# A small marker transfer and a wait for it ahead of eleven key loads of a decode attention kernel

## The chip, the cores and the metric

The kernel runs on one core of a Trainium2 chip. The metric is device time in microseconds, as the median of several runs. A profile is one execution of the program, recorded by the hardware profiler; its times count from the first instruction of the span.

## The reference

Two attention layers, A and B, take one new token for each of 4 batch entries, and their results are set side by side. Each has its own query weights `wq`, key and value caches and output weights `wo`. A reads its whole cache of 8192 positions, B only the last `W` = 2048.

```python
q = (x @ wq).reshape(B, Sq, Hq, Dh).transpose(0, 2, 1, 3)      # 32 heads of 128
k = jnp.repeat(k_cache, rep, axis=1)       # 8 key heads, rep = 4; B: k_cache[:, :, Sk - W:, :]
v = jnp.repeat(v_cache, rep, axis=1)
scores = jnp.einsum("bhqd,bhkd->bhqk", q, k) * (Dh ** -0.5)
p = softmax(scores, axis=-1)
o = jnp.einsum("bhqk,bhkd->bhqd", p, v)
return o.transpose(0, 2, 1, 3).reshape(B, Sq, Hq * Dh) @ wo
```

All tensors are bf16. The caches are large, and each of their elements is used for 4 query heads only.

## The kernel before

The work is cut into 20 units. Units 0 to 3 are B's, one per batch entry, with all 8 key heads. Units 4 to 19 are A's, each with two key heads of one batch entry. Every unit has 4 MB of keys and 4 MB of values. `K_sb` and `V_sb` have two slots each, and unit u uses slot u % 2.

For a unit, PE (TensorE) transposes the keys (L283, 16 groups of four), and DVE and ACT copy the transposed groups from PSUM (L299). PE forms the scores from them (L322), with scores of the first half in one of two banks SA and of the second half in SB. DVE takes maxima and differences, POOL the maximum over partitions (L441), ACT the exponentials (L469). PE then multiplies the values of the unit before with its probabilities (L338), and DVE divides by the sums (L491 for B, L504 for A); the semaphore of that step is called `otr`. Two units make a turn, and PE, ACT and DVE run the turns as a hardware loop. In each turn the output weights of one group of heads, 1 MB in `Wo_sb`, are multiplied in (L396), and DVE adds the product to `oacc` (L404, semaphore `ocp`).

All large loads are issued by SP (SyncE) at L566, in one queue, in the order that the loop from L753 writes down: for u = 1 to 20, the keys of unit u, then the values of unit u - 1, and, where u is even and at least 6, the 1 MB for `Wo_sb`. SP takes its list strictly in order (`emit`, L799), and a wait of one entry holds back all that follow. A key load of B comes in two halves, a value load of B in four quarters of 1 MB (L719 to L726). A's loads are whole, 4 MB each (L748), apart from the last unit's. What an entry waits for is that its slot is free:

```python
w = [("T", tjob_idx[(u - 2, 8 * q + 7)])] if u >= 2 else []                                  # keys of B, L721
w = [("otr", u - 2)] if kind == "V" else [("otr", u - 3)] if u >= 2 * T0P else [("T", tjob_idx[(u - 2, NJ - 1)])]   # A, L729
op("sp", dma(Wo_sb[:, :, :].rearrange("p r n -> p (r n)"), src), waits=[("ocp", tn - 1)], inc=("wo", tn))           # L761
```

`("T", ...)` is a transposition of the unit that used the slot before. The wait of one of A's loads stands at a semaphore increment just ahead of the load (L741). After the last value load SP issues eight pieces of `Wl_sb`, the last group of output weights, and at the end the outputs.

A transfer's semaphore counts 16, and `DMA_KEYS` (L162) names the keys that count so. `values` (L779) gives each key its count.

Of the kernel before, what the change touches and what calls it, by code (L numbers as in the profile page):

```python
# [6 lines left out]
BF16 = mybir.dt.bfloat16  # L7
# [7 lines left out]
def bass_concat_heads__gqa_block_cached__sliding_block_cached__decode_kernel(  # L15
# [23 lines left out]
    NSEG = 4  # L39
# [20 lines left out]
    WQ = [A_wq, B_wq]  # L60
    WO = [A_wo, B_wo]
# [11 lines left out]
    with ExitStack() as es:  # L73
        block = es.enter_context(nc.Block())

        def sb(name, shape, dt):
            return es.enter_context(nc.sbuf_tensor(name, shape, dt))

        def ps(name, n):
            return es.enter_context(nc.psum_tensor(name, [128, n], F32))  # L80

        def sm(name):
            return es.enter_context(nc.semaphore(name))
# [34 lines left out]
        OL = sb("OL", [128, C, Bn], BF16)  # L118
        oacc = sb("oacc", [Bn, D], F32)
        osb = sb("osb", [Bn, 2, D], BF16)  # L120
        dummy = sb("dummy_t", [128, 2], F32)
        SA = [ps("SA0", 512), ps("SA1", 512)]
        SB = ps("SB", 512)
# [2 lines left out]

        names = ["k0", "k1", "kh", "v0", "v1", "vl0", "vl1", "vl2", "wl0", "wl1", "wl2", "wl3", "wl4", "wl5", "wl6", "wl7", "x0", "x1", "w0", "w1", "wo",
                 "out0", "out1", "out2", "Tq", "Td", "Ta", "S", "PV", "Ed", "Ea", "Eq", "vs", "sub", "exp", "otr", "otp",
                 "ocp", "Ef", "fin0", "fin1", "ar1", "SM", "msk", "pset", "setup", "pm0", "pm1", "oc", "ocB", "mkb", "perm", "rq"]
        sems = {n: sm("s_" + n) for n in names}  # L130

        K_sbf = K_sb.bitcast(F32)
# [4 lines left out]
        tjob_idx, qp_idx, xt_idx, perm_idx, ot_idx, ol_idx, opj_idx = {}, {}, {}, {}, {}, {}, {}  # L137

        def sem_of(key):
            t = key[0]  # L140
            if t in ("K", "Kh"):
                return sems["k%d" % (key[1] % 2)]
            if t in ("V", "Vh"):
                return sems["v%d" % (key[1] % 2)]
            if t == "T":
                j = jobs[key[1]]
                return sems["Tq" if j["turn"] is None else "Td" if j["eng"] == "dve" else "Ta"]
            if t == "pm":
                return sems["pm%d" % key[2]]
            if t == "KH":  # L150
                return sems["kh"]
            if t in ("VL", "WL", "x", "out", "fin"):
                return sems["%s%d" % (t.lower(), key[1])]
            if t == "WQ":
                return sems["w%d" % key[1]]
            if t == "E":
                if jobs[key[1]]["turn"] is None:
                    return sems["Eq"]
                return sems["Ed"] if jobs[key[1]]["eng"] == "dve" else sems["Ea"]
            return sems["vs" if t in ("max", "maxc", "sum", "rcp", "os") else t]  # L160

        DMA_KEYS = ("K", "Kh", "KH", "V", "Vh", "VL", "WL", "x", "out", "WQ", "wo")  # L162

        plan = {e: [] for e in ("sp", "pe", "act", "dve", "pool")}
        turn = [None]
# [1 line left out]
        def op(eng, fn, waits=(), inc=None, bump=None):  # L167
            waits = list(waits)
            if not (eng == "pe" and turn[0] is not None):
                waits = [w for w in waits if w is not None]  # L170
            t = turn[0] if eng == "pe" or (eng in ("dve", "act") and turn[0] is not None and turn[0] >= T0P) else None
            plan[eng].append(dict(fn=fn, waits=waits, inc=inc, turn=t, bump=bump))
# [391 lines left out]
        def dma(dst, src):  # L564
            def fn(e):
                return e.dma_start(out=dst, in_=src)  # L566
            return fn
# [34 lines left out]
        for u in range(NU):  # L602
# [8 lines left out]
            for tok in TOK:  # L611
# [15 lines left out]
                if odd and tok in AFTER:  # L627
                    kind = AFTER[tok][0]
# [56 lines left out]
        for c in range(NC):  # L685
            w = [("VL", vch_of[c])]
# [18 lines left out]
        op("act", lambda act: act.activation(out=osb[:, 0, H2:D], in_=halves[1], func=ACTF.Copy), waits=[("fin", 1)], inc=("Ef",))  # L705
        op("act", dma(out[:, 0, H2:D], osb[:, 0, H2:D]), waits=[("Ef",)], inc=("out", 2))

        def kv_load(kind, u):
            un = units[u]
            cache = (KC if kind == "K" else VC)[un["P"]]  # L710
            buf = K_sb if kind == "K" else V_sb
            slot = u % 2
            if kind == "K" and slot == 1 and u < L:
                op("sp", lambda sp: sp.sem_inc(sems["kh"], 16), bump=(sems["kh"], 16, ("KH", u)))
            if un["P"] == 1:
                base = cache[un["b"], 0, SK - W:SK, :]
                hw = SK * DH
                n = NT // NPART[kind]
                for q in range(NPART[kind]):  # L719
                    if kind == "K":  # L720
                        w = [("T", tjob_idx[(u - 2, 8 * q + 7)])] if u >= 2 else []  # L721
                    else:
                        w = [("otr", u - 2)] if u >= 2 else [("T", tjob_idx[(1, 1)])] if u else [("T", qp_idx[(1, NQP - 1)])]
                    heads = HKV // NPART[kind]
                    src = bass.AP(tensor=base.tensor, offset=base.offset + q * heads * hw, ap=[[n * DH, W // n], [hw, heads], [1, n * DH]])
                    op("sp", dma(buf[:, slot, q * n:(q + 1) * n, :], src), waits=w, inc=(kind if q == NPART[kind] - 1 else kind + "h", u, q))  # L726
                return
            base = cache[un["b"], 2 * un["gp"], :, :]
            w = [("otr", u - 2)] if kind == "V" else [("otr", u - 3)] if u >= 2 * T0P else [("T", tjob_idx[(u - 2, NJ - 1)])]  # L729
            if kind == "V" and u == L:  # L730
                c0 = 0
                for i, n in enumerate(VCH):
                    t0, t1 = c0 * TC, (c0 + n) * TC
                    src = bass.AP(tensor=base.tensor, offset=base.offset + t0 * DH, ap=[[NT * DH, 32], [32 * NT * DH, 4], [1, (t1 - t0) * DH]])
                    op("sp", dma(buf[:, slot, t0:t1, :].rearrange("p t d -> p (t d)"), src), waits=w, inc=("VL", i))
                    c0 += n
                return
            src = bass.AP(tensor=base.tensor, offset=base.offset, ap=[[NT * DH, 32], [32 * NT * DH, 4], [1, NT * DH]])
            sem = sem_of((kind, u))
            bump = 16 * (NPART[kind] - 1)  # L740
            op("sp", lambda sp: sp.sem_inc(sem, bump), waits=w, bump=(sem, bump, None))  # L741
            if kind == "K" and u == L:
                for h in range(2):
                    t0 = h * NTH
                    src = bass.AP(tensor=base.tensor, offset=base.offset + t0 * DH, ap=[[NT * DH, 32], [32 * NT * DH, 4], [1, NTH * DH]])
                    op("sp", dma(buf[:, slot, t0:t0 + NTH, :].rearrange("p t d -> p (t d)"), src), inc=(kind, u, 0) if h == 0 else ("KH", u))
                return
            op("sp", dma(buf[:, slot, :, :].rearrange("p t d -> p (t d)"), src), inc=(kind, u, 0))  # L748

        for P in (1, 0):  # L750
            op("sp", dma(V_sb[:, 1 - P, :, :].rearrange("p t d -> p (t d)"), WQ[P].rearrange("(p c) n -> p (c n)", p=128)), inc=("WQ", P))
        kv_load("K", 0)
        for u in range(1, NU + 1):  # L753
            if u < NU:
                kv_load("K", u)
            kv_load("V", u - 1)
            tn = u // 2
            if u % 2 == 0 and tn in pieces:
                P, q = pieces[tn]
                src = WO[P][q * C * DH:(q + 1) * C * DH, :].rearrange("(p r) n -> p (r n)", p=128)  # L760
                op("sp", dma(Wo_sb[:, :, :].rearrange("p r n -> p (r n)"), src), waits=[("ocp", tn - 1)], inc=("wo", tn))  # L761
            if u == 16:
                op("sp", dma(out[:, 0, D:2 * D], osb[:, 1, :]), waits=[("ocB", 0)], inc=("out", 1))
# [17 lines left out]
        for eng in plan:  # L781
            for o in plan[eng]:
# [5 lines left out]
                if o["inc"] is not None:  # L788
                    key = o["inc"]
                    sem = sem_of(key)  # L790
                    amt = 16 if key[0] in DMA_KEYS else 1
                    counters[sem.name] = counters.get(sem.name, 0) + amt
# [143 lines left out]
```

## Time and profile before

| What | Value |
|---|---|
| Median of 3 runs | 439.15 us (438.97 to 439.83) |
| Profiled execution, its own time | 438.96 us |
| Its span | 437.0 us |
| PE busy | 365.0 us, 84% |
| DVE, ACT, POOL busy | 210.0, 195.0, 27.7 us |
| SP's DMA queue | 184.56 MB, 99.1% of 16 engines' span |
| HBM read | 184.56 MB |
| PE waiting for a key load (L283) | 34.4 us, 9 times |

Busy times are of one execution and add up over stages. The queue's share is the time that its packets took on the 16 DMA engines, against 16 times the span. The slices of the page cut the span into 40 equal parts; a digit is the busy share in tenths. In SP's order of time each row has the start, the duration of the issue on SP (not of the transfer), the line and the tile loaded; in the list of issues the last figure is the time from issue to landing. In a wait's row stand the engine and line that waited, what it waited for, the sum in us, how often, and the longest. In a row of a stretch stand its limits and length, the busy time of PE, PEld, DVE, ACT and POOL, the granted clock, the DMA share and the GB/s.

### The profile page before, as it was taken

How to read it: one execution, taken by the hardware profiler on the slowest of the kernel's cores; microseconds unless marked ns; L12 is line 12 of the kernel's file. 1: busy time of each engine (PE TensorE's matmuls, PEld its weight loads, DVE VectorE, ACT ScalarE, POOL GpSimd, SP SyncE). 2: the span in 40 equal slices, each digit the busy share in tenths (PEclk: the TensorE clock that was granted, in tenths of full speed). 3: DMA queues.
4: the chain of work that ended last, by engine and by line, in shares of the span. 5: the costliest groups of instructions: out<-in, count | busy, mean ns of one | idle time of the engine just before them, and what ended most of it. 6: DMA issues, size and time to landing. Idle time of an engine off the chain costs nothing.

```text
span 437.0 us, 15525 instructions
## 1 busy us (share of the span) xinstructions
PE 365.0 (84%) x7174; PEld 337.9 (77%) x7184; DVE 210.0 (48%) x406; ACT 195.0 (45%) x249; POOL 27.7 (6%) x88
## 2 busy tenths in 40 slices
PE   0168898998998959895989598969868996989996
PEld 0158897997997949795979588868868886979975
DVE  0004455664564634563456247525643563455651
ACT  1024473573653625371634254434534462536530
POOL 6100000000000000000000000000100000000000
PEclk9999999999999988999999899989996999799999
DMA  8999999999999999999999999999999999999996
GB/s 340 430 421 421 429 412 430 418 439 412 445 432 432 424 438 432 432 432 432 432 432 429 432 432 430 431 433 432 410 454 432 432 432 432 432 432 411 447 407 255
DMA packets 10996, 184.73 MB, mean 423 GB/s; under 512 B 1236, under 2 KB 2280, under 8 KB 2408
## 3 DMA queue, kind: packets, MB, share of 16 engines
q1 hardware_dynamic: 10960, 184.56, 99.1%
q8 instruction: 8, 0.13, 0.1%
q14 instruction: 4, 0.03, 0.0%
q10 hardware_dynamic: 24, 0.01, 0.0%
HBM read 184.56 MB, written 0.01 MB: 422 GB/s over the span
## 4 chain that ended last, share of the span: by engine, by line
PE 54%; DMA 40%; issue 2%; DVE 1%; SPq 1%; ACT 1%
DMA K_sb<-in_A_k_cache_dram 29%; PE KT L283 27%; PE OT L338 11%; DMA K_sb<-in_B_k_cache_dram 7%; PE SB L322 5%; PE SA L322 4%; DMA V_sb<-in_A_v_cache_dram 4%; PE KT L396 4%; PE SA L350 1%; PE KT L338 1%; SPq L566 1%; DVE oacc L404 1%; PE KT L263 1%; ACT KT_sb L299 1%; DVE OS L501 0%
## 5 line engine op out<-in xcount | busy, mean ns | idle before, releaser
L283 PE MATMUL KT<-identf,K_sb 128*128 128x128 f32 x1280 | 207.6, 296 | 44.1 <-DMA K_sb<-in_A_k_cache_dram 30.7
L299 ACT ACTIVATE KT_sb<-KT 128x1024 bf16<-128x1024 bf16 (+1 forms) x192 | 165.1, 881 | 120.6 <-PE KT L283 120.6
L283 PEld LDWEIGHTS KT<-identf,K_sb 128*128 128x128 f32 x1280 | 147.6, 150 | 49.3 <-DMA K_sb<-in_A_k_cache_dram 31.7
L299 DVE COPY KT_sb<-KT 128x512 int32<-128x512 int32 x160 | 110.5, 691 | 132.1 <-PE KT L283 130.7
L338 PE MATMUL OT<-PT,V_sb 128*128 128x64 bf16 x2560 | 78.1, 193 | 1.6 <-issue 1.1
L338 PEld LDWEIGHTS OT<-PT,V_sb 128*128 128x128 bf16 x2560 | 75.9, 98 | 1.8 <-issue 1.2
L469 ACT ACTIVATE PT<-Dt 128x512 bf16<-128x512 f32 x40 | 24.6, 630 | 84.0 <-DVE Dt L458 84.0
L322 PEld LDWEIGHTS SA<-RQc,KT_sb 128*128 128x128 bf16 x1280 | 56.9, 98 | 2.3
L322 PEld LDWEIGHTS SB<-RQc,KT_sb 128*128 128x128 bf16 x1280 | 51.1, 97 | 7.9 <-issue 4.4
L322 PE MATMUL SA<-RQc,KT_sb 128*128 128x16 bf16 x1280 | 56.4, 170 | 0.0
L322 PE MATMUL SB<-RQc,KT_sb 128*128 128x16 bf16 x1280 | 52.9, 170 | 0.0
L420 DVE TENSOR_REDUCE M<-SB 128x8 f32<-128x512 f32 (+1 forms) x20 | 13.8, 692 | 50.0 <-PE SB L322 50.0
L441 POOL PARTITION_ALL_REDUCE MB<-M1m x20 | 7.7, 387 | 334.3 <-DVE M1m L434 334.3
L396 PE MATMUL KT<-Wo_sb,OL 128*4 128x512 bf16 x80 | 18.9, 379 | 0.0
L201 PE MATMUL KT<-ident,x_sb 4*128 4x4 bf16 x8 | 0.6, 170 | 19.9 <-POOL identf L537 19.9
L201 PEld LDWEIGHTS KT<-ident,x_sb 4*128 4x128 bf16 x8 | 0.4, 112 | 20.1 <-issue 20.1
L476 DVE TENSOR_REDUCE LB<-SA 128x8 f32<-128x512 f32 (+1 forms) x20 | 13.7, 684 | 2.8 <-PE SA L350 2.8
L458 DVE TENSOR_TENSOR Dt<-SA,MBm 128x512 f32<-128x512 f32 x20 | 13.8, 692 | 0.7
L367 DVE TENSOR_TENSOR ORx<-KT,MSK 32x1024 bf16<-32x1024 bf16 x10 | 12.1, 1211 | 3.3 <-PE KT L362 3.3
L458 DVE TENSOR_TENSOR Dt<-SB,MBm 128x512 f32<-128x512 f32 x20 | 13.6, 681 | 0.0
L420 DVE TENSOR_REDUCE M<-SA 128x8 f32<-128x512 f32 (+1 forms) x20 | 13.6, 681 | 0.0
L350 PE MATMUL SA<-PT,onesb 128*128 128x128 bf16 x168 | 12.7, 218 | 0.0
(69 smaller groups left out, 118.0 us busy)
## 6 DMA issues: line engine op xcount, KB each, us to landing
K_sb<-in_A_k_cache_dram SPq DMA_DIRECT2D x15, 4096.0 KB, 22.5
V_sb<-in_A_v_cache_dram SPq DMA_DIRECT2D x15, 4096.0 KB, 30.3
K_sb<-in_B_k_cache_dram SPq DMA_DIRECT2D x8, 2048.0 KB, 23.6
V_sb<-in_B_v_cache_dram SPq DMA_DIRECT2D x16, 1024.0 KB, 18.4
V_sb<-in_B_wq_dram SPq DMA_DIRECT2D x1, 4096.0 KB, 12.5
V_sb<-in_A_wq_dram SPq DMA_DIRECT2D x1, 4096.0 KB, 21.8
Wo_sb<-in_B_wo_dram SPq DMA_DIRECT2D x4, 1024.0 KB, 11.9
K_sb<-in_A_k_cache_dram SPq DMA_DIRECT2D x2, 2048.0 KB, 17.5
```

What stands on the lines that cost most here:

```text
L283: ins = pe.transpose(out=bkf[:, pi * 128:(pi + 1) * 128], in_=K_sbf[:, slot, t0:t0 + 2, :].rearrange("p t d -> p (t d)"), identity=identf[ ...
L299: ins = e.tensor_copy(out=d, in_=r) if eng == "dve" else e.activation(out=d, in_=r, func=ACTF.Copy)
L322: ins = pe.matmul(out=stb[:, t % NTH * C:(t % NTH + 2) * C], lhsT=ktv[:, pi, :, e], rhs=RQc[:, u % 2, t // TS, e, :], start=(e == 0), stop ...
L338: ins = pe.matmul(out=otb[:, s * NW:s * NW + w], lhsT=V_sb[:, slot, t, :], rhs=PT[:, slot, t * C:t * C + w], start=(j == 0), stop=(j == n ...
L350: ins = pe.matmul(out=SA[u % 2][:, s * NM:(s + 1) * NM], lhsT=onesb[:, :], rhs=PT[:, u % 2, c0:c0 + NM], start=(i == 0), stop=(i == n - 1))
L367: return dve.tensor_tensor(out=ORx[:, :, :, :], in0=bk[0:NR, 0:128].rearrange("p (i o r) -> p r o i", o=1, r=C).broadcast_to([NR, C, C, 12 ...
L396: ins = pe.matmul(out=bk[0:Bn, 0:D], lhsT=OL[:, i, :], rhs=Wo_sb[:, i, :], start=(i == 0), stop=(i == C - 1))
L420: return dve.tensor_reduce(out=M1[:, h * n:(h + 1) * n].rearrange("p (s h) -> p s h", h=C), in_=bank[:, :].rearrange("p (s j h) -> p s h j ...
L441: return pool.partition_all_reduce(MB[:, 0:n], M1m[:, 0:n], channels=128, reduce_op=ReduceOp.max)
L458: return dve.tensor_tensor(out=Dt[:, h * NTH * C:(h + 1) * NTH * C].rearrange("p (s j h) -> p s j h", s=Sh, h=C), in0=bank[:, :].rearrange ...
L469: return act.activation(out=PT[:, u % 2, a:b], in_=Dt[:, a:b], func=ACTF.Exp, scale=scale)
L476: return dve.tensor_reduce(out=LB[:, 0:n].rearrange("p (s h) -> p s h", h=C), in_=SA[u % 2][:, 0:NSEG * NM].rearrange("p (s j h) -> p s h ...
```

## The change

A new tile `rs_sb` of 16 rows of 32 elements (64 bytes a row, 1 KB) takes a small transfer from A's `wo`, which nothing reads. Its key is `rs`, on one semaphore. `mark(u)` puts it in SP's list for the units in `MARKS`; `passed()` gives the next key load a wait for it.

- Units 0 to 3: the marker goes ahead of the last quarter of the unit's values, and the next key load (of units 2 to 5) waits for it. For units 2 and 3 it is the first half of the keys that waits.
- Units 5, 7, 9, 11, 13, 15 and 17: the marker goes ahead of the entry for `Wo_sb`, its wait for `ocp` included, and the key load of the unit two later (7, 9, 11 to 19) waits for it. The load waits for the marker beside its old wait.

Key loads of units 6, 8, 10 to 18 have no marker. The order of all other transfers, and every other engine's list, is as before. The lines of the new kernel lie one further from the new tile on, and 17 further after `kv_load` and the loop.

```diff
+        rs_sb = sb("rs_sb", [16, 32], BF16)
...
-        DMA_KEYS = ("K", "Kh", "KH", "V", "Vh", "VL", "WL", "x", "out", "WQ", "wo")
+        DMA_KEYS = ("K", "Kh", "KH", "V", "Vh", "VL", "WL", "x", "out", "WQ", "wo", "rs")
...
+        MARKS = (0, 1, 2, 3, 5, 7, 9, 11, 13, 15, 17)
+        marked = []
+
+        def mark(u):
+            if u in MARKS:
+                op("sp", dma(rs_sb[:, :], WO[0][0:16, 0:32]), inc=("rs", u))
+                marked.append(u)
+
+        def passed():
+            return [("rs", marked.pop())] if marked else []
+
         def kv_load(kind, u):
...
                     if kind == "K":
-                        w = [("T", tjob_idx[(u - 2, 8 * q + 7)])] if u >= 2 else []
+                        w = ([("T", tjob_idx[(u - 2, 8 * q + 7)])] if u >= 2 else []) + passed()
                     else:
                         w = [("otr", u - 2)] if u >= 2 else [("T", tjob_idx[(1, 1)])] if u else [("T", qp_idx[(1, NQP - 1)])]
+                        if q == NSEG - 1:
+                            mark(u)
...
             w = [("otr", u - 2)] if kind == "V" else [("otr", u - 3)] if u >= 2 * T0P else [("T", tjob_idx[(u - 2, NJ - 1)])]
+            if kind == "K":
+                w = w + passed()
...
             if u % 2 == 0 and tn in pieces:
                 P, q = pieces[tn]
+                mark(u - 1)
                 src = WO[P][q * C * DH:(q + 1) * C * DH, :].rearrange("(p r) n -> p (r n)", p=128)
                 op("sp", dma(Wo_sb[:, :, :].rearrange("p r n -> p (r n)"), src), waits=[("ocp", tn - 1)], inc=("wo", tn))
```

More of the change, by code (lines that the diff above doesn't have):

```diff
@@ L128, in bass_concat_heads__gqa_block_cached__sliding_block_cached__decode_kernel @@
                  "out0", "out1", "out2", "Tq", "Td", "Ta", "S", "PV", "Ed", "Ea", "Eq", "vs", "sub", "exp", "otr", "otp",
-                 "ocp", "Ef", "fin0", "fin1", "ar1", "SM", "msk", "pset", "setup", "pm0", "pm1", "oc", "ocB", "mkb", "perm", "rq"]
+                 "ocp", "Ef", "fin0", "fin1", "ar1", "SM", "msk", "pset", "setup", "pm0", "pm1", "oc", "ocB", "mkb", "perm", "rq", "rs"]
         sems = {n: sm("s_" + n) for n in names}
```

## The prediction

> **What bounds the kernel now.** I read the page first, its slices and its DMA queues:
>
> ```profile
> span 437.0 us, 15525 instructions
> ...
> DMA  8999999999999999999999999999999999999996
> GB/s 340 430 421 421 429 412 430 418 439 412 445 432 432 424 438 432 432 432 432 432 432 429 432 432 430 431 433 432 410 454 432 432 432 432 432 432 411 447 407 255
> ...
> q1 hardware_dynamic: 10960, 184.56, 99.1%
> ```
>
> The DMA row is at 9 from the second slice to the last but one, and one queue, SP's, carries all of it. PE is busy for 84%. A queue that is never empty sets the end; every microsecond in which it runs dry is lost.
>
> The chain of waits puts 54% on PE, and its pieces are PE work without a break from 33.88 to 140 us. That is no contradiction: the chain follows a key load back to its issue, and the issue to PE, though the load then stood in the queue. So I looked at the order of time on SP, for one turn, and at SP's own waits:
>
> ```profile
> 159.25 0.54 SPq L566 DMA_DIRECT2D K_sb<-in_A_k_cache_dram  x1
> 159.89 0.55 SPq L566 DMA_DIRECT2D V_sb<-in_A_v_cache_dram  x1
> 183.97 0.33 SPq L566 DMA_DIRECT2D Wo_sb<-in_B_wo_dram  x1
> 184.48 0.54 SPq L566 DMA_DIRECT2D K_sb<-in_A_k_cache_dram  x1
> 185.12 0.55 SPq L566 DMA_DIRECT2D V_sb<-in_A_v_cache_dram  x1
> 201.46 0.54 SPq L566 DMA_DIRECT2D K_sb<-in_A_k_cache_dram  x1
> ```
>
> ```profile
> SPq L566 <- DVE oacc L404: 137.0, 6, 23.8
> SPq L741 <- DVE ON L504: 94.6, 6, 16.5
> ```
>
> K of unit 9, issued at 184.48, is needed at once but lands at 205.3, 20.8 us later. Its own 4.19 MB and the 1.05 MB of Wo before it take 9.74 + 2.5 us, so V of unit 7 had 8.5 us to go at the issue. That is the depth of the queue at its shallowest in a turn, and what the change spends. The rates come from two views, the stretch of the first loads and the issues:
>
> ```profile
> 13.30:23.00 9.70, 2.69 (x96) 2.67 (x97) 0.65 (x4) 0.78 (x4) 1.74 (x8) 1.00 1.00 429
> ```
>
> ```profile
> V_sb<-in_B_wq_dram SPq DMA_DIRECT2D x1, 4096.0 KB, 12.5
> V_sb<-in_A_wq_dram SPq DMA_DIRECT2D x1, 4096.0 KB, 21.8
> Wo_sb<-in_B_wo_dram SPq DMA_DIRECT2D x4, 1024.0 KB, 11.9
> ```
>
> Two 4 MB loads issued 0.44 us apart land 9.74 us apart (0.80 + 12.5 and 1.24 + 21.8): that is the price of 4.19 MB in a full queue. The first, into an empty queue, took 12.5, so start and completion together cost 2.76.
>
> The trace's records of single packets add the rest. A 32 KB packet takes 1.218 us, a 16 KB one 0.612, an 8 KB one 0.312, a 512 B one 0.026, a completion 0.009. The 16 engines do not run level: V of unit 7 ends between 190.46 and 192.65, a lag of 2.19 us which builds up over the first 58 us and then stands still.
>
> **What the Trainium skill says.** "DMA: Bandwidth & Descriptors", section "Queues, rings and completion order": on each engine a queue's descriptors are consumed in ring order, and the completion increment lands only after that engine's earlier writes. The trace agrees as far as it goes: loads land in the order of issue. The section "Why a DMA increments its semaphore by 16 and not by 1": the full count needs every engine that the transfer uses, and 16 rows use all 16. So the marker lands when the last engine has passed it. "Anatomy of one DMA": a semaphore is waited for on the issuing sequencer, not by the DMA engines, and a transfer has about 2 us fixed, mostly completion (a fit for another issue path). Here completion is shorter: 0.37 us from the last completion packet to the semaphore, at the first load and at the output alike.
>
> **The change, part by part.** *Removed:* nothing. *Added:* 11 transfers of 16 rows of 64 bytes, and 11 waits on SP. On each engine a marker is one small packet and a completion, 0.035 us by the 512 B row; I take 0.04, so 11 x 0.04 = 0.4 us, all on the stream that sets the end. Their issues (0.29 to 0.37 us on SP, as for the outputs) fall while SP has 9 us and more to spare: four just before a last V quarter, seven before a wait for L404.
>
> *Moved:* the key load, from the end of SP's other waits to the landing of the marker. In the turn shown that is from 184.48 to about 193.2. Behind it on SP stand V of unit 8 (then issued at about 193.9, with 12 us of K before it) and K of unit 10, which waits until 201.46 anyway. So nothing else is late, and the cost is what happens between marker and key load. From the passing of the last engine, at 192.69:
>
> - landing 0.37; SP's waking 0.02 to 0.13 (Wo goes out 0.02 after DVE's end; PE starts on K 0.13 after its semaphore), I take 0.08; one semaphore increment 0.10 (the gap between the issues at 184.48 and 185.12, less 0.54)
> - from the issue to the first packets 1.05 to 1.60 on fifteen engines at the first load (issued at 0.80, packets from 1.84 to 2.40)
> - sum: packets can start 1.6 to 2.15 us after the marker.
>
> On the last engine the short transfer (Wo, or a V quarter: both 8 packets of 8 KB) covers 8 x 0.312 = 2.50 us. So on the engine that sets the end the load comes 0.35 to 0.9 us before it is empty. The engines that are ahead by up to 2.19 us run dry, but that only uses up their lead.
>
> What no row shows is whether a load that comes so late joins without a gap. Into an empty queue, the first packets took 1.3 to 2.23 us in place of 1.218: 0.1 to 1.0 us of filling. Were all of that paid, full rate would begin 2.15 to 3.0 us after the marker, and since a load lands with its slowest engine, the stream would lose 3.0 - 2.5 = 0.5 us per marker. If filling hides behind the short transfer, it loses 0. Below nothing I see no way. I take 0.2, nearer to 0, since the requests are out while 8 KB packets still move. Then 11 x (0.2 + 0.04) = 2.6 us: the span goes from 437.0 to 439.6, and with 1.96 us around it (438.96 - 437.0) to 441.6 against the profiled execution. The median of the runs is 0.19 above that execution, so 441.8.
>
> The four markers of units 0 to 3 are no cheaper. PE runs behind the key loads there (no wait for K in the chain from 33.88 on), with K of unit 2 landed some 13 us before its turn, but their gaps stay in the stream and arrive at K of unit 7.
>
> **Rivals.** A difference under 0.2% (0.9 us) can't be told from none; 0.08 us per marker is the border.
>
> *Hidden*: the key load joins in time, only the packets cost: 439.15 + 0.4 = 439.6. For it speaks the 0.35 to 0.9 us in hand; against it the fill of up to 1.0. A marker that passed V out of turn would end here too, as the wait would never be the last.
>
> *Late*: the marker's completion takes the skill's 2 us in a loaded queue, not 0.37. Packets then start 3.25 to 3.8 after it, 0.75 to 1.3 past the cover; with 0.3 of filling I take 1.3 per marker: 11 x 1.34 = 14.7, so 453.9. Against it: 0.37 us for a load with the queue full behind it.
>
> *Faster*: bringing the engines level lets the B part move at the later rate. From 54 to 106 us the stretches moved 418, 422 and 428 GB/s, later ones about 431. B's 33.6 MB of K and V would take 77.8 us instead of 79.3 at 423, 1.5 us less, hence 438.1 with the packets. It decides from 428 GB/s on. Against it: the 8 KB packet costs 0.312 us where a quarter of a 32 KB one is 0.305, and the change leaves packets as they are. Nothing else could be faster: the stream has no gap to close.
>
> **How the numbers follow.** The restart cost at 0.08 to 0.5 per marker: 0.58, its own range 440.4 to 445.1. Hidden 0.29, late 0.08, faster 0.05. The range holds the first two and a little past the upper bound, 438.8 to 446.5, which leaves out faster and late, 0.13, and some of the uncertainty of the bounds. Slower 0.58 + 0.08 = 0.66, same 0.29, faster 0.05.
>
> **What would show it.** SP's waits have a row of some 11 waits for the marker's DMA, about 8 to 9 us each, and L404 stays beside it. The marked key loads land about 12 us after issue, not 21 to 23; the unmarked ones stay above 20. Wo goes out at about the old times plus the gaps so far. The queue's share falls from 99.1% to 97 or 98%, as leading engines stand still. The lag at the end of a load, 2.2 us now, falls below 1.5. The landings of K of units 7, 9, 11 and 13 are now 41.3 us apart (164.0, 205.3, 246.7, 288.0); I expect 41.4 to 41.8, hidden shows no more than 41.4, late 42.6. PE's idle time before K grows by what the stream loses. I am wrong if the gap on the last engine is not what I bound: the fill under load is the unmeasured term.

## The result

The changed kernel takes 461.21 us (median of 6 runs, 454.9 to 465.29), the kernel before 439.19 (438.97 to 439.83). The ratio is 1.043, with a 95% interval from 1.035 to 1.050; it leaves out the two longest runs of the changed kernel, one of which is the profiled one. The forecast was 441.8, in a range up to 446.5. So the direction was right and the size was not: 22 us by the medians and 19 by the ratio, in place of 2.6, and single runs that lie 10 us apart, where those of before lie within 1.

The page of the kernel after, with the lines that answer to those shown of before (span, share of the DMA engines and GB/s in 40 slices, SP's queue):

```profile
span 460.5 us, 15538 instructions
...
DMA  9999999999999999989998999899999979997995
GB/s 365 403 424 418 379 417 367 418 372 402 403 430 433 387 433 424 441 356 436 430 436 362 445 421 409 339 436 436 382 407 416 450 291 444 416 450 306 431 425 211
...
q1 hardware_dynamic: 11312, 184.57, 95.3%
```

Before, nearly all slices from the fourteenth on were at some 430 GB/s; now one in each turn falls to between 291 and 387. The same bytes flow at about the same rate between these dips. SP's waits of the kernel after:

```profile
SPq L567 <- DVE oacc L405: 146.1, 6, 25.0
SPq L757 <- DMA rs_sb<-in_A_wo_dram: 94.8, 9, 16.7
...
SPq L823 <- DMA rs_sb<-in_A_wo_dram: 36.8, 2, 22.3
```

The markers are waited for 11 times, as expected, and the row for Wo's wait for DVE is still there. SP's order of time in the turn of unit 11, and the issues with their time to landing, after and before:

```profile
234.59 0.35 SPq L567 DMA_DIRECT2D Wo_sb<-in_B_wo_dram  x1
244.16 0.54 SPq L567 DMA_DIRECT2D K_sb<-in_A_k_cache_dram  x1
244.84 0.54 SPq L567 DMA_DIRECT2D V_sb<-in_A_v_cache_dram  x1
252.11 0.54 SPq L567 DMA_DIRECT2D K_sb<-in_A_k_cache_dram  x1
```

```profile
K_sb<-in_A_k_cache_dram SPq DMA_DIRECT2D x15, 4096.0 KB, 15.0
V_sb<-in_A_v_cache_dram SPq DMA_DIRECT2D x15, 4096.0 KB, 24.0
```

```profile
K_sb<-in_A_k_cache_dram SPq DMA_DIRECT2D x15, 4096.0 KB, 22.5
V_sb<-in_A_v_cache_dram SPq DMA_DIRECT2D x15, 4096.0 KB, 30.3
```

The key load goes out 9.6 us after Wo here (8.8 to 9.7 over the seven turns), where the prediction has about 9.2. But it then takes longer to land: the row's 15.0 is the median of marked and unmarked loads together, and the marked ones of units 7 to 17 take 13.2 to 15.0 us, where about 12 was forecast. Where the missing time is, the trace's records of landings say. In a full queue 4 MB of keys land 9.72 us after the load ahead of them, and the half load of unit 19 4.9. Behind Wo, in the seven marked turns of A, they land later by 2.05, 1.2, 2.95, 2.15, 3.05, 2.8 and 2.5 us, 16.7 in all; behind a last quarter of B's values by 1.65, 2.75, 0.55 and 1.55, 6.5 in all. Together 23.2 us, and the span has grown by 23.5. All other loads land at the old distance. The loss is at the eleven places of the change and nowhere else, but it is 2.1 us at each, not 0.2, and it varies.

### The profile page after: what moved, and what is told of

It reads as the page before. It is cut to its first block, busy times and chain, and to the rows that moved or that the text cites. A ratio compares the mean times of both kernels' runs of the same rounds, so it can differ in the third digit from the quotient of the medians.

```text
span 460.5 us, 15538 instructions
## 1 busy us (share of the span) xinstructions
PE 368.0 (80%) x7174; PEld 340.3 (74%) x7184; DVE 209.9 (46%) x406; ACT 195.0 (42%) x249; POOL 27.6 (6%) x88
## 3 DMA queue, kind: packets, MB, share of 16 engines
q1 hardware_dynamic: 11312, 184.57, 95.3%
## 4 chain that ended last, share of the span: by engine, by line
DMA 54%; PE 24%; PEld 15%; issue 4%; SPq 2%; PEldq 1%; DVE 0%; ACT 0%
DMA rs_sb<-in_A_wo_dram 30%; DMA K_sb<-in_A_k_cache_dram 12%; PE KT L284 11%; DMA K_sb<-in_B_k_cache_dram 7%; PEld KT L284 7%; PE OT L339 5%; DMA V_sb<-in_A_v_cache_dram 5%; PEld OT L339 3%; PEld SA L323 2%; SPq L567 2%; PEld SB L323 2%; PE SB L323 2%; PE SA L323 2%; PE KT L339 1%; PEldq L905 1%
## 5 line engine op out<-in xcount | busy, mean ns | idle before, releaser
L284 PE MATMUL KT<-identf,K_sb 128*128 128x128 f32 x1280 | 209.9, 298 | 62.7 <-DMA K_sb<-in_A_k_cache_dram 49.0
L284 PEld LDWEIGHTS KT<-identf,K_sb 128*128 128x128 f32 x1280 | 149.5, 151 | 68.2 <-DMA K_sb<-in_A_k_cache_dram 50.1
```

Of the source, the lines that this page charges most:

```text
L284: ins = pe.transpose(out=bkf[:, pi * 128:(pi + 1) * 128], in_=K_sbf[:, slot, t0:t0 + 2, :].rearrange("p t d -> p (t d)"), identity=identf[ ...
```

## The experiments

Three words are used from here on. The *cover* is the work that stands in the queue behind the marker, in us of transfer: what the engines still have to do once the marker has passed. The *restart* is the time from the marker's passing of the last engine until the key load runs at full rate. *Late* is how much later than in a full queue the key load lands, counted from Wo's landing.

Theory 1 is the one of the prediction: a wait spends the depth of the queue, and what is lost is the restart less the cover that the short transfer gives. Its rivals: the small transfers disturb the stream; a wait for all 16 engines has a price of its own, whatever the cover.

**Markers without waits.** The markers stay, each in its own columns of a larger tile; no load waits for one.

```diff
-            return [("rs", marked.pop())] if marked else []
+            return []
```

> All eleven markers go out where the change puts them (each into its own columns of the tile), but no key load waits for one. Theory 1 (the wait spends the queue's depth; what is lost is the time from the marker's passing to the key load at full rate, less the cover of the short transfer): no wait, no loss, only 11 x 0.04 us of packets, 439.2 to 440.0. Rival, the small transfers themselves disturb the stream (2 us each): the time of the changed kernel, 455 to 465.

Measured: 439.36 us, ratio 1.0003 (0.9995 to 1.0012). The markers themselves cost nothing that can be measured, not even the 0.4 us that I gave them.

**Only A's seven markers.**

```diff
-        MARKS = (0, 1, 2, 3, 5, 7, 9, 11, 13, 15, 17)
+        MARKS = (5, 7, 9, 11, 13, 15, 17)
```

> Only the seven markers of layer A (units 5 to 17), with their waits; the four of layer B and their waits are gone. In the profile of the changed kernel the seven landings of a key load behind Wo come 1.2 to 3.1 us late, 16.7 in all, the four of B 0.5 to 2.8, 6.4 in all. Theory 1: the losses add up, so 439.2 + 16.7 = 456, within 452 to 459. Rival, B's markers bring the engines out of step once and A only inherits it: below 446.

Measured: 454.26 us (450.81 to 456.76), ratio 1.032 (1.026 to 1.039). The losses add up. The rest of the study works with these seven, since they all stand in the same place.

**Twice the cover.** The value load ahead of Wo is issued in two parts, with the marker between.

```diff
+            if kind == "V" and u in MARKS:
+                for i, (t0, t1) in enumerate(((0, 3 * NT // 4), (3 * NT // 4, NT))):
...
+                    if i == 0:
+                        mark(u)
```

> A's seven markers as in the run with these alone, but the value load ahead is cut in 3/4 and 1/4, and the marker stands between the parts: behind it come 1 MB of values and 1 MB of Wo, 4.9 us of cover in place of 2.5. Theory 1 with a slowest engine that is back at full rate 2.5 + 2.4 = 4.9 us after the marker: 0 to 0.4 us per marker, 439.2 to 442. Rival, a wait for all 16 engines costs its 2.4 us however deep the queue is: 454 to 459.

Measured: 440.03 us, ratio 1.0024 (1.0015 to 1.0033). SP still waits seven times for a marker:

```profile
SPq L757 <- DMA rs_sb<-in_A_wo_dram: 47.5, 7, 8.1
```

Yet the six whole key loads land 9.71 to 9.73 us after Wo, and the half load 4.90, as in the kernel before. So the wait as such costs nothing; the depth behind it decides.

**No cover.** The marker moves behind Wo.

```diff
-                mark(u - 1)
                 src = WO[P][q * C * DH:(q + 1) * C * DH, :].rearrange("(p r) n -> p (r n)", p=128)
                 op("sp", dma(Wo_sb[:, :, :].rearrange("p r n -> p (r n)"), src), waits=[("ocp", tn - 1)], inc=("wo", tn))
+                mark(u - 1)
```

> A's seven markers behind Wo instead of ahead of it: nothing in the queue covers the key load. Theory 1: each loses 2.5 us more, 7 x (2.4 + 2.5) = 34 us, 473 (465 to 478). Rival, a price per wait whatever the cover: 454 to 459. If only one late engine makes the loss at 2.5 us of cover, and all restart alike from an empty queue, about 7 x 3.2 = 22 us, 462.

Measured: 462.01 us (461.88 to 463.03), ratio 1.053. That is 3.3 us per marker, and the key loads land 2.8 to 3.6 us late, 3.1 in the mean. Theory 1 in its plain form wanted 473. Four stretches of one microsecond in this run, around one marker, and SP's issue there:

```profile
242.00:243.00 1.00, 1.00 (x24) 0.98 (x22) 0.33 (x2) 0.73 (x1) 0.00 (x0) 1.00 0.42 165
243.00:244.00 1.00, 1.00 (x24) 0.99 (x21) 0.65 (x1) 0.66 (x2) 0.00 (x0) 1.00 0.00 0
244.00:245.00 1.00, 1.00 (x19) 0.64 (x17) 0.00 (x0) 0.66 (x1) 0.00 (x0) 1.00 0.73 197
245.00:246.00 1.00, 1.00 (x40) 1.00 (x39) 0.48 (x1) 0.00 (x0) 0.00 (x0) 1.00 0.79 328
```

```profile
243.43 0.54 SPq L567 DMA_DIRECT2D K_sb<-in_A_k_cache_dram  x1
```

For a whole microsecond nothing moves. This measures the restart by itself: from the passing of the last engine to the marker's landing 0.62 us; SP 0.07; from the issue to the first packets 1.3 us on the first engines and 1.5 to 2.3 on the others, often in two groups of eight; and the early packets take 1.7 to 2.2 us instead of 1.21. The engines end the load within 0.25 to 1.0 us of each other.

The sum, 3.1, leaves 0.6 with 2.5 us of cover. But there 2.2 was lost. The packet records of the run with 2.5 us of cover show why. From the second marker on mostly one engine is late: 15 engines end the key load close together, and the last one 1.2 to 2.5 us after them. In the turn of unit 11 the last Wo packet ends at 240.88, fifteen first key packets begin from 240.33 to 240.94, and the sixteenth begins at 242.46 and takes 2.35 us. The records do not name the engine of a packet, but the turn of unit 13 in the changed kernel leaves one only: fifteen first key packets begin from 289.98 to 290.21, while the sixteenth engine is still at its last Wo packet, which ends at 290.51, and its own first key packet begins at 291.78 and takes 2.13. So the late engine is the one that was last with Wo. In the turns of these two kernels in which it is over a microsecond behind, its first key packet begins 0.8 to 2.4 us after its last Wo packet. From this comes **theory 2**: an engine that the new descriptors (the load's entries in the engine's queue) meet just as it runs dry restarts later than an empty one.

**Other covers.** Behind the marker stand an eighth of the values and Wo (3.7 us), half of Wo (1.24) or three quarters of Wo (1.86), by cuts like the one above. For half of Wo:

```diff
+                op("sp", dma(dst[:, 0:2048], src[:, 0:2048]), waits=[("ocp", tn - 1)], inc=("wo", tn, "h"))
+                mark(u - 1)
+                op("sp", dma(dst[:, 2048:4096], src[:, 2048:4096]), inc=("wo", tn))
```

> A's seven markers, the value load ahead cut in 7/8 and 1/8 with the marker between: 0.5 MB of values and 1 MB of Wo behind it, 3.7 us of cover. With no cover a marker lost 22.9 / 7 = 3.3 us, with 2.5 us of cover 2.2. Theory 1, one restart time of 3.3 us less the cover: nothing lost, 439 to 440. Theory 2, the engine that is last and still at work when the load's descriptors come restarts later than an idle one (full rate 2.5 + 2.2 = 4.7 us after the marker): 7 x 1.0 us, 446 (443 to 448).

> A's seven markers in the middle of the Wo load, which is cut in two halves: 1.24 us of cover. Theory 2: all engines are empty before the load's descriptors come (1.4 to 2.3 us after the marker has landed), so all restart alike and lose 3.3 - 1.2 = 2.0 us, 7 x 2.0 = 14.3, 453.4 (451 to 455), no more than with 2.5 us of cover. Rival, the loss falls evenly from 3.3 without cover to 2.2 at 2.5 us: 2.7 us each, 458.

> A's seven markers after the first quarter of Wo: 1.86 us of cover. Theory 2: the engines are empty 1.2 us after the marker's landing, just before the descriptors come; 3.3 - 1.9 = 1.4 us each, 449 (447 to 452), less than with 2.5 us of cover. Rival, an even fall: 2.45 us each, 456.

Measured: 444.55 us, 457.37 and 456.38. By the whole time the first is within what theory 2 expected, and the other two are outside it and at what its rival expected. By the landings it looks different:

| cover, us | time, us | per marker by time, us | key load late by, mean of seven, us |
|---|---|---|---|
| 0 | 462.01 | 3.3 | 3.1 |
| 1.24 | 457.37 | 2.6 | 1.8 |
| 1.86 | 456.38 | 2.5 | 1.6 |
| 2.48 | 454.26 | 2.2 | 2.4 |
| 3.7 | 444.55 | 0.8 | 0.6 |
| 4.9 | 440.03 | 0.1 | 0.0 |

(The landings are of the one profiled execution; that at 2.48 was one of the longer, and in a shorter one, shown further down, the loads were late by 1.8 in the mean.) Up to 1.86 us the key load is late by 3.1 less the cover, to 0.3 us, and the engines stay within 1.1 us of each other at each of its landings. At 2.48 that sum gives 0.6, and the load is late by 1.8 to 2.4, no less than at 1.24. At 1.24 and 1.86, however, Wo in its two parts took 3.0 and 3.3 us in the mean instead of 2.5, which is most of the rest of the time. That time is lost ahead of the marker, not in the restart: from the landing of the values to that of the marker it takes 1.40 and 0.85 us in the first turn, and 1.95 to 2.2 and 1.7 to 2.0 in the six after it.

**The cuts alone.** Three kernels without markers, with Wo cut in halves, Wo cut after a quarter, and the values cut as for 4.9 us:

> No markers and no waits; only the Wo load in two halves, as in the run with 1.24 us of cover. There Wo's two landings took 3.1 us together in place of 2.5, and the key load behind them lost 1.84, not 2.6. If the cut alone costs 0.6 us a turn: 439.2 + 7 x 0.6 = 443.4 (442 to 445), and the marker's own loss at this cover is 1.8 to 2.0, as theory 2 had it. If the cut is free: 439 to 440, and the even fall stands.

> No markers and no waits; only the Wo load cut after the first quarter, as in the run with 1.86 us of cover, where Wo's two landings took 3.4 us together and the key load behind lost 1.56. If the cut alone costs 0.95 us a turn: 445.8 (444 to 447.5). If it is free: 439 to 440.

> No markers and no waits; only the value loads of units 5 to 17 cut in 3/4 and 1/4, as in the run with 4.9 us of cover, which took 0.9 us more than before. If the cut is that: 440.0. If the markers are: 439.2.

Measured: 439.62, 439.64 and 439.68, each with a ratio of 1.001. The cuts cost 0.5 us in all, so they are free, and by the expectations that leaves the even fall standing: by the whole time theory 2 had 1.24 and 1.86 us of cover wrong. Wo's slower parts come only with the markers. What the traces show is that with the markers the engines stand almost level there from the second turn on (0.5 to 1.6 us), without them 1.5 to 2.7 us apart, and that with Wo in halves a tenth of the 4 KB packets then take from 0.29 to 0.6 us, where without markers none takes over 0.17. Something like it ends two other runs with level engines: with no cover the last 512 KB of values land 1.4 us later against the load ahead than in the kernel before, and in the run with 16 increments below the first piece of `Wl_sb` 1.3 us. That level engines get in each other's way on short packets is a reading of this and was not tried. Of the 0.9 us at 4.9 us of cover, half is the cut.

**A marker on eight rows,** whose semaphore waits for eight of the engines:

> A's seven markers in their place ahead of Wo, but of 8 rows, so that the semaphore waits for 8 of the 16 engines. Theory 2: if the late engine is one of the other eight, the load comes earlier for it and its delay isn't renewed: at most 3.3 - 2.5 = 0.8 us per marker, 439 to 445. If it is one of the eight, no change: 451 to 457. Rival, all engines lose alike whatever the marker waits for: 451 to 457.

Measured: 449.83 us (448.05 to 452.15), between the two expectations. The key loads are late by 0.5 in two of the turns and by 1.6 to 2.1 in the others. In the trace each such marker has 8 packets in place of 16. The run doesn't say which engine is late, and it decides nothing.

**A later issue.** The sharpest test of theory 2 delays the key load further, by increments of a semaphore that nothing uses, put between the marker's wait and the load.

```diff
             op("sp", lambda sp: sp.sem_inc(sem, bump), waits=w, bump=(sem, bump, None))
+            if kind == "K" and any(x[0] == "rs" for x in w):
+                for _ in range(16):
+                    op("sp", lambda sp: sp.sem_inc(sems["dl"], 1))
```

> A's seven markers ahead of Wo as the change has them, and then 16 increments of an unused semaphore on SP between the marker's wait and the key load, which delay its issue by some 0.7 us (0.04 to 0.06 each). Theory 2: the late engine (a first key packet up to 1.6 us after its last Wo packet, and 2.3 us long) arises because the load's descriptors come just as it runs dry. With the delay all engines are dry before, restart alike and lose 3.1 + 0.7 - 2.5 = 1.3 us per marker instead of 2.2 to 2.4: 448 (446 to 451), a later issue and a shorter time. Rival, one restart time however the engines stand: 0.7 us more per marker, 459.

Measured: 451.95 us (451.5 to 452.79). The delay was larger than planned: the load goes out 1.02 us after the marker's landing (1.5 and 1.4 in two turns), where it was 0.07. The time is just above the stated range; with 1.0 instead of 0.7 the same sum gives 1.6 us per marker, and the landings show 1.64. The rival was far off. Since the run without delay spreads widely, both were taken again on one chip, with a longer delay beside them:

> A's seven markers and waits, as in the run with these alone, taken again on the same chip as the two with a delay. That run: 454.3, from 450.8 to 456.8. Theory 2: the same, with single runs far apart, as in each turn one engine may come late or not; landings of the key load behind Wo with a spread of 2 us over the engines.

> The kernel with 16 increments ahead of the key load, taken again. There the delay was 1.03 us and the loss per marker 1.6, as 3.1 + 1.0 - 2.5 says, with the 16 engines' landings within 0.3 to 0.9 us. Theory 2: 450.5 to 453, shorter than the one without delay, single runs close together. Rival, the first comparison was chance: 7 us longer than the one without delay.

> 32 increments instead of 16: 2.06 us of delay. Theory 2: all engines are empty in both, so the further 1.03 us is paid in full: 7 x 1.03 = 7.2 more than with 16, 459 (458 to 460.5). If the delay itself cost little because something else sets the time: below 455.

Measured: 454.48 us without delay (ratio 1.0337, 1.0309 to 1.0364), 452.02 with 16 increments (1.0288, 1.0274 to 1.0302), 459.38 with 32 (1.0457, 1.0443 to 1.0471). The last two are within what theory 2 expected. Single runs overlap: 451.98 to 455.57 without delay, 451.54 to 452.37 with 16 increments. The profiled execution without delay was a short one (span 450.5 us, 450.0 with 16 increments), and still it shows the difference in the landings, 12.6 us late in all against 11.1. Here are the seven key landings behind Wo from the traces of these two runs (time, distance to Wo's landing, spread over the 16 engines, distance of the last engine from the last but one; the seventh load is half as long):

```
no delay                   16 increments
165.12 10.69 0.95 0.42     166.11 11.68 0.94 0.54
208.40 11.64 1.58 0.89     209.30 11.44 0.28 0.01
252.38 12.35 2.44 2.17     252.15 11.22 0.38 0.11
296.46 12.46 2.58 1.69     295.07 11.24 0.59 0.09
340.23 12.18 2.29 1.95     337.77 11.04 0.32 0.01
382.01 10.13 0.44 0.01     380.52 11.09 0.26 0.08
419.96  6.32 1.13 0.15     418.84  6.58 0.55 0.04
```

Where the last engine is within 0.9 us of the others, the load without delay loses 0.4 to 1.9 us; where it is 1.7 to 2.2 behind, 2.5 to 2.7. Not every engine that is met this way comes late: in the sixth turn the last Wo packet ends among the arrivals too, 1.94 us after the load's issue, and all 16 first key packets have begun 0.3 us later. What decides between the two is not known.

With the load sent a microsecond later, when every engine is empty, the late engine is gone, the distances are alike, and by the medians the kernel is 2.5 us shorter. The second step of the delay, 0.9 us more in the mean, is then paid in full: 7.4 us for seven markers by the time, 7.0 by the landings. The delay also leaves the engines almost level from turn to turn, and no run separates that from their being empty.

## Why the prediction was wrong

*What bounds the kernel*: right. The same bytes, the same rate between the gaps, and every gap goes straight into the end. The 9.74 us for a load of 4 MB come from rounded times (the two landings lie 9.68 us apart, later ones 9.72), and nothing hangs on them. Nothing behind the wait on SP became late: value loads and unmarked key loads land at the old distances.

*Part one, packets, 0.4 us*: too much; nothing that can be measured.

*The path from marker to first packet, 1.6 to 2.15 us*: too short. The landing takes some 0.62 us, not the 0.37 that I read from a large load and an output; only SP was quicker, 0.07 in place of 0.18. The issue takes 1.3 to 2.3 us to the first packets, not 1.05 to 1.6. I had taken the first load of the kernel, another access pattern whose issue lasts 0.38 us, where a key load's lasts 0.54, and of that load only fifteen engines: the sixteenth has its first packet at 2.94, 2.14 us after the issue, and it is the slowest engine that counts. Both were in the profile.

*Filling, "I take 0.2, nearer to 0, since the requests are out while 8 KB packets still move"*: wrong. In these runs filling hides only where the descriptors come well before an engine is dry. At 3.7 us of cover they reach the last engine 0.7 us or more before, and some first packets still take 2 to 2.4 us; at 4.9 it is hidden. With the measured terms all paid, the restart is 3.1 us and the loss 0.6 per marker, 446 in all. That would have been at the edge of the range, so these terms alone do not make the miss.

*"Were all of that paid, ... the stream would lose 3.0 - 2.5 = 0.5 us per marker"*: this is the step that failed. It was given as the upper bound, and takes for granted that an engine still at work when the load's descriptors come restarts no later than an empty one. It can restart later. The 2.5 us of the short transfer put the last engine's end among the arrivals of the new descriptors (1.7 to 1.9 us after the issue, where they come from 1.3 to 2.3), and in most turns it then restarts 0.8 to 2.4 us after its end, with a first packet of 1.7 to 2.5 us. The lag of 2.2 us that I had seen in the profile and let lie as lead that is used up is renewed at most markers by the engine that is last. This makes some 2.2 per marker of 0.6, and the wide spread: a marker costs 0.4 to 3 us, by whether an engine comes late. What inside the engine delays it no run shows.

*The rivals*: "late" was nearest in time (453.9), for a reason that is not the case: the marker's landing is 0.62 us, not 2. "Hidden" is what happens at 4.9 us of cover. "Faster" had no basis: level engines were no faster, and on short packets slower.

*Signs*: the count of the waits, DVE's row beside them and the unmarked loads above 20 us came as stated. The sizes did not: the waits are 12.0 us each in place of 8 to 9, the queue's share is 95.3% in place of 97 to 98, and K of units 7, 9, 11 and 13 land 42.6, 44.3 and 43.7 us apart in place of 41.4 to 41.8. The lag "below 1.5" reached 3.0, and that was the sign of what I had missed.

## What to carry to other kernels

Before a wait is put ahead of a load in a stream that sets the end, count what is left in the queue when the wait ends, and hold it against a restart measured for that very load, with the fill: here 3.1 us from an empty queue, and 4.9 us of queued work to lose nothing. A cover a little shorter than the restart (here 2.5 us) is the worst place to be careless, because the loss is then neither the difference nor steady. A transfer lands with its slowest engine, so read the spread of the 16 landings too, not only the mean share.

## What the runs showed that I had not expected

- A load issued 1.0 us later made the kernel 2.5 us shorter by the medians (454.48 to 452.02); all 16 engines were then empty and restarted alike.
- Seven waits with 2.48 us of work behind them cost no less at the key load than with 1.24 us (2.4 and 1.8 us each in two executions, against 1.8, by landings).
- A load cut in two costs nothing in a full queue (0.5 us for seven), but its parts took 0.5 to 1.15 us a turn longer where a marker had brought the engines level before.
